# Loading the last 64 rows of three weight matrices: one transfer over 128 partitions, or two over 64

## The chip, the cores and the metric

The kernel runs on one core of a Trainium2 chip. The metric is device time in microseconds (us) of one execution; lower is better. A core has a matrix engine (PE in the profile), a vector engine (DVE), a scalar engine (ACT), GpSimd (POOL) and SyncE (SP). SP computes nothing here: it issues every transfer between the main memory and the on-chip buffer (SBUF, 128 partitions). Sixteen DMA engines carry the transfers.

## The reference

Two attention layers and two dense layers in turn, for one new token in each of 8 sequences. Both attention layers use the same weights and the same caches, and so do both dense layers.

```python
# x: 8 x 1 x 448 (bf16); 16 query heads, 8 key/value heads of size 256; the last 1024 positions of a cache of 4096
def A(x, k_cache, v_cache, wq, wo):          # wq 448 x 4096, wo 4096 x 448
    q = (x @ wq) per head; scores = q @ k.T * 256 ** -0.5
    return (softmax(scores) @ v) @ wo
def B(x, w1, w2):                             # w1 448 x 1792, w2 1792 x 448
    return silu(x @ w1) @ w2
x = x + A(layernorm(x)); x = x + B(layernorm(x))
x = x + A(layernorm(x)); x = x + B(layernorm(x))
```

## The kernel before

The first attention layer, the first dense layer and the second attention layer are computed sequence by sequence (b = 0 to 7), so that each K and V block is loaded once and used by both attention layers. The second dense layer comes once at the end, for all sequences together. In the code `layer1(b)` is the first attention layer of a sequence, `layer2(b)` the first dense layer (`chain`) and the second attention layer.

**Weights.** The inner dimension of wq, w1 and of each quarter of w2 is 448 = 3 x 128 + 64. The first 384 rows fill three column blocks of all 128 partitions. The last 64 rows fill a narrower block: its left half (output columns of the first half) lies in partitions 0 to 63, its right half in partitions 64 to 127. Two transfers of 64 partitions each bring that block, in each of `load_wq` (L411), `load_w1` (L419) and `load_w2` (L434).

**Loads.** All loads go through SP's queue in the order of the program: x, wq (three large and two small), the eight K blocks of sequence 0, w2 (four and two), wo (one), the eight V blocks of sequence 0, w1 (one and two), then for each next sequence eight K (L468) and eight V blocks (L480 and L474). A block is 512 KB. There are `R` = 30 slots for them; a load beyond the thirtieth waits until the PE has read the block that was in its slot.

**Compute.** DVE transposes each K block in its slot (L899). PE multiplies the queries by it (L639, in `scores`), DVE takes the maximum (L645) and turns it (L651 to L655), ACT takes the exponential (L659), PE transposes the result (L664) and multiplies it by V (L696, in `pv_rows`). PE then multiplies by wo (L765). In `chain`, PE multiplies by w1 (L518) and w2 (L793), and then by wq for the second layer's queries (L806). The very first use of wq is the projection for all eight sequences at the start (L511). Each transfer has a semaphore of its own; a product with wq, w1 or w2 waits for all transfers of that matrix (`WQ_R`, `W1_R`, `W2_R`).

**Order.** A planner (`Plan.schedule`) sets the order of the tasks on PE, DVE, ACT and POOL before the program is built. It simulates the engines with durations written in tables, and takes the ready task with the highest rank plus an entry of `BIAS`. `HOLD` says how long it holds an engine for a more urgent task, `PE_SCALE` stretches the PE's durations. The `rate` of a transfer (bytes per us) is the planner's guess of its speed and goes nowhere else. On the chip, each engine runs its list in that order, and semaphores make it wait.

Of the kernel before, what the change touches and what calls it, by code (L numbers as in the profile page):

```python
# [20 lines left out]
       "act:exp": 0.38, "act:oev": 0.30, "act:pTev": 0.20, "act:qrow": 0.51, "act:rowb": 0.50, "act:tanh": 0.22,  # L21
       "pool:pow": 0.53, "pool:pow8": 1.63}
SP_ISSUE, DMA_FIRST, DMA_LAST = 0.47, 1.2, 2.2
HOLD, PE_SCALE = 0.709, 1.049
BIAS = {"dve.KT.a": -15.4, "dve.max.a": -69.3, "dve.mT.a": -77.8, "act.exp.a": 32.3, "pe.l.a": 54.2,
        "pe.xinit.a": 20.0, "act.rsum.a": 23.2, "act..a": 109.1, "pe.oT.a": 45.0, "pe.wo.a": -2.4, "pe.stat.b":
        141.6, "pe.qturn.b": 64.2, "pe.qsel.b": 103.4, "pe.S1.0.b": 42.7, "pe.S1.1.b": 21.5, "dve.mg.c": -66.5,
        "act.exp.c": 37.9, "pe.l.c": -84.2, "pe.PV1.0.1.c": -85.8, "pe.PV1.0.3.c": 4.6, "pe.oT.c": -76.3,
        "dve.oTev.c": -102.8, "pe.PV1.1.2.c": -78.3}


class Task:
# [13 lines left out]
class Plan:  # L46
# [10 lines left out]
    def add(self, eng, fns, reads=(), writes=(), dur=0.1, prio=0.0, name="", n_bytes=0, dma_key=None):  # L57
        if not isinstance(fns, (list, tuple)):
            fns = [fns]
        if eng == "pool":  # L60
            writes = list(writes) + ["pool_serial"]
        t = Task(eng, list(fns), dur, prio, name, n_bytes)
        t.idx = len(self.tasks)
        t.sem = dma_key
        deps = {}

        def dep(o, raw):
            if o is not t:
                deps[o.idx] = (o, raw or (deps[o.idx][1] if o.idx in deps else False))

        for k in reads:
            if k in self.last_w:
                dep(self.last_w[k], True)
            if k[0] == "bank":
                for r in self.readers.get(k, ()):
                    if r.eng != eng:
                        dep(r, False)
        for k in writes:
            if k in self.last_w:
                dep(self.last_w[k], True)  # L80
            for r in self.readers.get(k, ()):
                dep(r, False)
        for k in reads:
            if k not in writes:
                self.readers.setdefault(k, []).append(t)
        for k in writes:
            self.last_w[k] = t
            self.readers[k] = []
        t.deps = deps
        self.tasks.append(t)  # L90
        return t

    def schedule(self):
# [15 lines left out]
        for t in reversed(tasks):  # L109
            r = max([u.rank + lag(t, u, raw) for u, raw in succ[t.idx]], default=0.0)  # L110
            t.rank = occ[t.idx] + r
            if t.eng == "sp":
                t.rank += DMA_FIRST + DMA_LAST
                if t.idx in following:
                    t.rank = max(t.rank, occ[t.idx] + following[t.idx].rank)
        urgency = [t.rank + BIAS.get(t.kind, 0.0) for t in tasks]

# [132 lines left out]
def bass_interleave_layers__sliding_block_cached__dense_activation_silu__decode_kernel(  # L250
    nc, A_x, A_k_cache, A_v_cache, A_wq, A_wo, B_x, B_w1, B_w2, out
):
    NB, Sq, D = A_x.shape
    _, HKV, SK, DH = A_k_cache.shape
    HD = A_wq.shape[1]
    H = HD // DH
    F = B_w1.shape[1]
    W = min(4096, max(256, SK // 4))
    S0 = SK - W
    P = 128  # L260
    assert NB == 8 and Sq == 1 and DH == 256 and H == 16 and HKV == 8 and W == 1024 and D == 448 and F == 1792
    KC = 4
    HD2, F2 = HD // 2, F // 2
# [13 lines left out]
    wq_sb = sb("wq_sb", [P, 3 * HD + HD2], BF16)  # L277
    wo_sb = sb("wo_sb", [P, NCH * DP], BF16)
    w1_sb = sb("w1_sb", [P, 3 * F + F2], BF16)
# [64 lines left out]
    def bk(i):  # L344
        return [("bank", i)]
# [7 lines left out]
    def act(fn, reads, writes, dur, prio, name=""):  # L353
        add("act", fn, reads=reads, writes=writes, dur=dur - LAT["act"], prio=prio, name=name)

    def pe(fns, reads, writes, shape, prio, name=""):

        n = len(fns) if isinstance(fns, (list, tuple)) else 1
        add("pe", fns, reads=reads, writes=writes, dur=n * max(0.0265, shape[0] / shape[1] / 2230.0), prio=prio,
            name=name)  # L360
# [40 lines left out]
    def dma(fn, writes, n_bytes, key, reads=(), rate=411.2e3):  # L401
        add("sp", fn, reads=reads, writes=writes, n_bytes=n_bytes, dma_key=key, dur=n_bytes / rate, name=key)
# [3 lines left out]
    def load_wq():  # L406
        for c in range(3):
            dma(lambda e, c=c: e.dma_start(wq_sb[:, c * HD:(c + 1) * HD], A_wq[c * P:(c + 1) * P, :]),
                [("wq", c)], P * HD * 2, "wq%d" % c, rate=410e3)
        for h in range(2):  # L410
            dma(lambda e, h=h: e.dma_start(wq_sb[64 * h:64 * h + 64, 3 * HD:], A_wq[3 * P:D, h * HD2:(h + 1) * HD2]),  # L411
                [("wq", 3 + h)], 32 * HD * 2, "wq%d" % (3 + h), rate=250e3)

    def load_w1():
        dma(lambda e: e.dma_start(w1_sb[:, 0:3 * F].rearrange("p (c n) -> p c n", c=3),
                                  B_w1[0:3 * P, :].rearrange("(c p) n -> p c n", p=P)),
            [("w1", 0)], 3 * P * F * 2, "w1", rate=390e3)
        for h in range(2):
            dma(lambda e, h=h: e.dma_start(w1_sb[64 * h:64 * h + 64, 3 * F:], B_w1[3 * P:D, h * F2:(h + 1) * F2]),  # L419
                [("w1", 1 + h)], 32 * F * 2, "w1%d" % h, rate=250e3)  # L420

    def load_wo():
        dma(lambda e: e.dma_start(wo_sb[:].rearrange("p (c n) -> p c n", n=DP)[:, :, 0:D],
# [2 lines left out]
    def load_w2():  # L426
        rows = w2_sb[:].rearrange("p (c n) -> p c n", n=DP)[:, :, 0:D]
        parts = B_w2.rearrange("(j r) n -> j r n", j=4)
        for j in range(4):
            dma(lambda e, j=j: e.dma_start(rows[:, 3 * j:3 * j + 3, :],  # L430
                                           parts[j, 0:3 * P, :].rearrange("(c p) n -> p c n", p=P)),
                [("w2", j)], 3 * P * D * 2, "w2%d" % j, rate=400e3)
        for h in range(2):
            dma(lambda e, h=h: e.dma_start(rows[64 * h:64 * h + 64, 12:14, :],  # L434
                                           parts[h:4:2, 3 * P:D, :].rearrange("j p n -> p j n")),
                [("w2", 4 + h)], P * D * 2, "w2%d" % (4 + h), rate=250e3)

    WO_R = ["wo"] + [("wo_s", g) for g in range(8)]
    W2_R = [("w2", j) for j in range(6)] + [("w2_s", g) for g in range(4)]
# [1 line left out]
    def row_sums(w, key, groups, prio):  # L441

        needs = ([("w2", j) for j in range(6)] if key == "w2" else [key]) + H8
        for g, (i0, i1) in enumerate(groups):
# [10 lines left out]
            else:  # L455
                for i in range(i0, i1):
# [2 lines left out]
                        accum_out=row[:, i - i0:i - i0 + 1]), needs, ["rowb", ("sums", key, g)], 0.75, prio, "rsum")  # L459
                act(lambda e, view=view, n=n, row=row: e.activation(view[:, :, D], row[:, 0:n], ACTF.Copy),  # L460
                    [("sums", key, g)], [(key + "_s", g)], 0.22, prio)
    WQ_R = [("wq", c) for c in range(KC + 1)]
    W1_R = [("w1", c) for c in range(3)]

    slot_of = {}

# [38 lines left out]
    def proj(bank_i, col, outs, lhs, half, rhs, n):  # L505

        fns = []
        for o in outs:
            for i in range(KC):
                r = rhs(xcol(i, o // half))  # L510
                fns.append(lambda e, o=o, i=i, r=r: e.matmul(  # L511
                    bank[bank_i][:, col + (o - outs[0]) * n:col + (o - outs[0] + 1) * n], lhs(o, i), r,
                    start=(i == 0), stop=(i == KC - 1)))
        return fns

    def up(x, nb, bi, col, reads, prio, fresh):
# [3 lines left out]
            tile_position=(0, 32 * j), skip_group_check=True) for c in range(KC) for j in range(4)],  # L520
           reads + W1_R, bk(XB) + ["part"], (D, 4), prio, "w1")
        if nb == 1:
# [48 lines left out]
    def start_rows(prio):  # L571
# [18 lines left out]
        pe(proj(YB, 0, range(NCH), wq_l, 16, lambda i: xh[:, i, :], 2 * NB),  # L590
           H8 + WQ_R, bk(YB), (2 * NB, 1), prio, "q1")
        yv = bank[YB][:, 0:2 * NCH * NB].rearrange("p (c n) -> p c n", n=2 * NB)
# [190 lines left out]
    def chain(b, prio):  # L783
# [20 lines left out]
        for k2 in range(2):  # L804
# [4 lines left out]
                start=(c == 0), stop=(c == KC - 1), tile_position=(0, 32 * j), skip_group_check=True)  # L809
                for c in range(KC) for j in range(4)], ["xbt"] + WQ_R, bk(wb), (512, 4), prio, "wq")  # L810
            act(lambda e, wb=wb: e.activation(qrow[:], bank[wb][:], ACTF.Copy),  # L811
# [56 lines left out]


    load_wq()  # L870
    start_rows(-10)

# [4 lines left out]
    def pump():  # L877

        while n_load[0] < len(seq) and (n_load[0] < R or seq[n_load[0] - R] in freed):
            x = seq[n_load[0]]  # L880
            slot_of[x] = n_load[0] % R
            n_load[0] += 1
            (load_k if x[1] == "k" else load_v)(slot_of[x], x[0], x[2])
            if x == (0, "k", 7):
                load_w2()
                load_wo()
            if x == (0, "v", 7):
                load_w1()
# [81 lines left out]
```

## Time and profile before

| | |
|---|---|
| median of 3 runs | 269.94 us (268.32 to 271.89) |
| the profiled execution | 270.87 us |
| its span, first to last instruction | 268.7 us |
| busy: PE, DVE, ACT, POOL | 190.6, 151.1, 89.1, 12.8 us |
| moved by the DMA engines | 78.21 MB, mean 291 GB/s |
| mean granted PE clock | 0.942 of full speed |

The profiled execution is 2.17 us longer than its span. All times below with a start are counted from the start of the span. The 40 slices of the page's second part are 6.7 us each. A row of stretches gives the length of the stretch, the busy time of each engine with the number of its instructions in brackets, the PE's clock, the share of the 16 DMA engines' time in which packets were under way, and the GB/s moved. A transfer's "landing" is the time from its issue by SP to its completion.

### The profile page before, as it was taken

To read this page: it belongs to the slowest core of one execution; us is meant where nothing else is said; L and a number is where in the kernel's file an instruction comes from. 1 tells how busy PE (TensorE), PEld (TensorE's weight loads), DVE (VectorE), ACT (ScalarE), POOL (GpSimd) and SP (SyncE) were. 2 spreads that over 40 slices of the span, in tenths; PEclk is the share of its full clock that TensorE was granted. 3 is DMA by queue.
4 is the path that set the end of the run, shared out by engine and by line. 5 is a ranking of instruction groups with operands and counts; after the bars stand their busy time and mean duration, and the time that the engine had idled before them with its cause. 6 is when DMAs were issued, how large, how long until landed. Compare 5 with 4: busy or idle time off the path is not lost.

```text
span 268.7 us, 8339 instructions
## 1 busy us (share of the span) xinstructions
PE 190.6 (71%) x3697; PEld 99.1 (37%) x3697; DVE 151.1 (56%) x410; ACT 89.1 (33%) x241; POOL 12.8 (5%) x25
## 2 busy tenths in 40 slices
PE   0062212398599977986997699689969986987663
PEld 0051100133345344444544444344435444433320
DVE  6369548619824973794686488449645862112211
ACT  2001347543133414433342443215233423230221
POOL 1200000000000000000000000000000000000020
PEclk9999999999959999999999999999988997995795
DMA  6999999999999999998999999899989984000000
GB/s 250 337 404 371 298 342 348 369 347 402 351 365 409 362 295 387 395 348 261 410 377 303 395 400 350 235 378 388 329 246 406 371 258 144 2 2 2 0 2 1
DMA packets 50227, 78.21 MB, mean 291 GB/s; under 512 B 2304, under 2 KB 41104, under 8 KB 49808
## 3 DMA queue, kind: packets, MB, share of 16 engines
q1 hardware_dynamic: 50192, 77.68, 83.6%
q8 instruction: 29, 0.48, 0.7%
q14 instruction: 6, 0.05, 0.1%
HBM read 77.67 MB, written 0.01 MB: 289 GB/s over the span
## 4 chain that ended last, share of the span: by engine, by line
PE 54%; SPq 19%; DMA 9%; DVE 8%; ACT 6%; issue 2%; POOL 1%; DVEq 0%; ACTq 0%
PE bank L696 11%; PE bank L639 10%; DMA slot<-in_A_k_cache_dram 9%; SPq L480 6%; PE bank L806 5%; SPq L430 5%; PE bank L772 5%; PE bank L765 5%; SPq L468 3%; SPq L474 3%; PE bank L518 3%; DVE mseg L645 2%; ACT qbd L659 2%; PE bank L793 2%; ACT qrow L811 2%
## 5 line engine op out<-in xcount | busy, mean ns | idle before, releaser
L899 DVE STREAM_TRANSPOSE slot<-slot 128x512 uint32<-128x512 uint32 x128 | 81.9, 684 | 9.3 <-DMA slot<-in_A_k_cache_dram 9.2
L696 PE MATMUL bank<-slot,pT_sb 128*2 128x256 bf16 x960 | 43.0, 307 | 9.6 <-DMA slot<-in_A_v_cache_dram 8.6
L639 PE MATMUL bank<-slot,qbd 128*8 128x256 bf16 x1024 | 42.0, 296 | 10.6 <-DVE slot L899 6.4
L696 PEld LDWEIGHTS bank<-slot,pT_sb 128*2 128x2 bf16 x960 | 21.6, 89 | 23.7 <-DMA slot<-in_A_v_cache_dram 9.0
L639 PEld LDWEIGHTS bank<-slot,qbd 128*8 128x8 bf16 x1024 | 21.8, 88 | 21.6 <-DVE slot L899 7.9
L659 ACT ACTIVATE qbd<-bank,mseg 128x256 bf16<-128x256 f32 x32 | 13.2, 472 | 41.7 <-DVE mseg L655 27.5
L664 PE MATMUL bank<-ident,qbd 128*128 128x128 bf16 x64 | 7.2, 249 | 23.4 <-ACT qbd L659 23.4
L704 ACT ACTIVATE qbd<-bank 128x256 bf16<-128x256 f32 x32 | 12.3, 384 | 29.4 <-PE bank L696 24.0
L765 PE MATMUL bank<-wo_sb,oT 128*1 128x449 bf16 x256 | 20.0, 368 | 0.0
L772 PE MATMUL bank<-wq_sb,cols_b 128*128 128x512 bf16 x64 | 19.4, 384 | 0.0
L645 DVE TENSOR_REDUCE mseg<-bank 128x1 f32<-128x256 f32 x32 | 13.2, 415 | 10.9 <-PE bank L639 10.4
L750 POOL TENSOR_TENSOR rhalf<-var,nhalf 128x1 f32<-128x1 f32 x16 | 8.7, 543 | 222.4 <-ACT var L748 222.4
L710 DVE TENSOR_TENSOR oT<-bank,l_sb 128x16 bf16<-128x16 f32 (+1 forms) x32 | 5.8, 195 | 22.2 <-PE bank L706 22.2
L608 ACT ACTIVATE qbd<-bank,mask 128x128 bf16<-128x128 f32 x32 | 12.2, 381 | 17.2 <-PE bank L603 16.4
L806 PE MATMUL bank<-wq_sb,xbt 128*1 128x512 bf16 x256 | 17.4, 393 | 0.6 <-DVE xbt L739 0.6
L677 DVE TENSOR_REDUCE l_sb<-bank 128x16 f32<-128x64 f32 x16 | 3.3, 205 | 24.4 <-PE bank L672 24.4
L664 PEld LDWEIGHTS bank<-ident,qbd 128*128 128x128 bf16 x64 | 4.3, 109 | 27.4 <-ACT qbd L659 26.9
L811 ACT ACTIVATE qrow<-bank 128x512 bf16<-128x512 f32 x16 | 9.6, 597 | 9.6 <-PE bank L806 9.6
L449 DVE TENSOR_REDUCE qbd<-wo_sb 128x5 f32<-128x2240 bf16 x4 | 9.7, 2479 | 2.6 <-DMA wo_sb<-in_A_wo_dram 2.6
L622 DVE TENSOR_TENSOR qbd<-bank,maskr 128x256 bf16<-128x256 f32 x16 | 6.8, 422 | 7.6 <-PE bank L617 7.6
L778 ACT ACTIVATE qrow<-bank 128x449 bf16<-128x449 f32 x8 | 4.4, 550 | 18.5 <-PE bank L765 18.5
L778 ACT ACTIVATE qrow<-bank,rhalf 128x449 bf16<-128x449 f32 x8 | 5.1, 640 | 11.3 <-PE bank L793 11.3
(133 smaller groups left out, 204.6 us busy)
## 6 DMA issues: line engine op xcount, KB each, us to landing
slot<-in_A_k_cache_dram SPq DMA_DIRECT2D x64, 512.0 KB, 10.5
slot<-in_A_v_cache_dram SPq DMA_DIRECT2D x64, 512.0 KB, 8.7
wo_sb<-in_A_wo_dram SPq DMA_DIRECT2D x1, 3584.0 KB, 17.9
wq_sb<-in_A_wq_dram SPq DMA_DIRECT2D x3, 1024.0 KB, 6.9
w_sb<-in_B_w_dram SPq DMA_DIRECT2D x4, 336.0 KB, 16.0
w_sb<-in_B_w_dram SPq DMA_DIRECT2D x1, 1344.0 KB, 11.5
wq_sb<-in_A_wq_dram SPq DMA_DIRECT2D x2, 256.0 KB, 10.3
w_sb<-in_B_w_dram SPq DMA_DIRECT2D x4, 112.0 KB, 9.5
```

The source lines that it names most:

```text
L430: dma(lambda e, j=j: e.dma_start(rows[:, 3 * j:3 * j + 3, :], parts[j, 0:3 * P, :].rearrange("(c p) n -> p c n", p=P)), [("w2", j)], 3 * P ...
L480: dma(lambda e: e.dma_start(slots[s][:, :].rearrange("v (j n) -> v j n", j=4), src.rearrange("j (v uh) d -> v j (uh d)", uh=2)), [("slot", ...
L639: fns.append(lambda e, cb=cb, par=par, j=j, kvh=kvh, kv=kv: e.matmul(bank[sc][32 * j:32 * j + 8, k2 * 256:(k2 + 1) * 256], qbd[qi][:, kvh, ...
L645: dve(lambda e: e.tensor_reduce(mseg[layer][:, k2:k2 + 1], bank[sc][:, k2 * 256:(k2 + 1) * 256], AX.X, ALU.max, negate=True), bk(sc), [("m ...
L659: act(lambda e, k2=k2: e.activation(e_sb[ei][:, k2, :, :].rearrange("p uh (jj ul) -> p uh jj ul", ul=4), bank[sc][:, k2 * 256:(k2 + 1) * 2 ...
L696: fns.append(lambda e, q=q, uh=uh, j=j, vv=vv: e.matmul(bank[ob][32 * j:32 * j + 2, c0:c0 + DH], pT_sb[ei][:, k2 * 2 + uh, j * 8 + 2 * q:j ...
L704: act(lambda e: e.activation(o_t, bank[ob][:, c0:c0 + DH], ACTF.Copy), bk(ob), [("qbd", ei, k2)], 0.42, prio, "oev")
L765: fns.append(lambda e, i=i, c=c, kvh=kvh: e.matmul(bank[XB][32 * c:32 * c + 1, 0:D1], oT1[:, i % 2, i // 2:i // 2 + 1], wo_sb[:, i * DP:i ...
L772: pe([lambda e: e.matmul(bank[SC[1]][:], zero_b.broadcast_to([P, P]), wq_sb[:, 0:512], start=False, stop=True, skip_group_check=True) for ...
L806: pe([lambda e, j=j, c=c, k2=k2, wb=wb: e.matmul(bank[wb][32 * j:32 * j + 1, :], xbt[:, xcol(c, k2):xcol(c, k2) + 1], wq_sb[:, c * HD + (( ...
L811: act(lambda e, wb=wb: e.activation(qrow[:], bank[wb][:], ACTF.Copy), bk(wb), ["rowb"], 0.55, prio, "qrow")
L899: dve(lambda e, v=v: e.transpose(v, v), [("slot", s)], [("slot", s)], 0.67, prio, "KT")
```

## The change

Each pair of 64-partition transfers for wq and w1 becomes one transfer over all 128 partitions. In main memory the two halves of a row lie next to each other, so the source is addressed as (half, row, column): 2 x 64 x 2048 elements for wq, 2 x 64 x 896 for w1. For w2 there are still two transfers, but each now covers 128 partitions and one column block, with a source of 2 x 64 x 448, instead of 64 partitions and two column blocks. The lists of semaphores to wait for become shorter by one for wq and w1. The planner's `BIAS`, `HOLD`, `PE_SCALE` and rates change as well.

```diff
-HOLD, PE_SCALE = 0.709, 1.049
-BIAS = {"dve.KT.a": -15.4, "dve.max.a": -69.3, "dve.mT.a": -77.8, "act.exp.a": 32.3, "pe.l.a": 54.2,
...
+HOLD, PE_SCALE = 0.659, 1.047
+BIAS = {"dve.KT.a": -21.1, "pe.S0.0.a": -50.7, "dve.max.a": -100.8, "dve.mT.a": -157.3, "act.exp.a": 42.6,
...
-        for h in range(2):
-            dma(lambda e, h=h: e.dma_start(wq_sb[64 * h:64 * h + 64, 3 * HD:], A_wq[3 * P:D, h * HD2:(h + 1) * HD2]),
-                [("wq", 3 + h)], 32 * HD * 2, "wq%d" % (3 + h), rate=250e3)
+        dma(lambda e: e.dma_start(wq_sb[:, 3 * HD:], A_wq[3 * P:D, :].rearrange("r (h n) -> h r n", h=2)),
+            [("wq", 3)], 64 * HD * 2, "wq3")
...
-        for h in range(2):
-            dma(lambda e, h=h: e.dma_start(w1_sb[64 * h:64 * h + 64, 3 * F:], B_w1[3 * P:D, h * F2:(h + 1) * F2]),
-                [("w1", 1 + h)], 32 * F * 2, "w1%d" % h, rate=250e3)
+        dma(lambda e: e.dma_start(w1_sb[:, 3 * F:], B_w1[3 * P:D, :].rearrange("r (h n) -> h r n", h=2)),
+            [("w1", 1)], 64 * F * 2, "w11", rate=390e3)
...
-        for h in range(2):
-            dma(lambda e, h=h: e.dma_start(rows[64 * h:64 * h + 64, 12:14, :],
-                                           parts[h:4:2, 3 * P:D, :].rearrange("j p n -> p j n")),
-                [("w2", 4 + h)], P * D * 2, "w2%d" % (4 + h), rate=250e3)
+        for i in range(2):
+            dma(lambda e, i=i: e.dma_start(rows[:, 12 + i, :], parts[2 * i:2 * i + 2, 3 * P:D, :]),
+                [("w2", 4 + i)], P * D * 2, "w2%d" % (4 + i), rate=350e3)
...
-    WQ_R = [("wq", c) for c in range(KC + 1)]
-    W1_R = [("w1", c) for c in range(3)]
+    WQ_R = [("wq", c) for c in range(KC)]
+    W1_R = [("w1", c) for c in range(2)]
```

Lines behind the change have numbers smaller by 4 in the changed kernel (L895 is what was L899). SP's queue before, from the first wq transfer to the second group of K blocks; the shape is that of the destination, partitions first:

```order
L408 DMA wq_sb<-in_A_wq_dram 128x4096 x3
L411 DMA wq_sb<-in_A_wq_dram 64x2048 x2
L468 DMA slot<-in_A_k_cache_dram 128x2048 x8
L430 DMA w_sb<-in_B_w_dram 128x3x448 x4
L434 DMA w_sb<-in_B_w_dram 64x2x448 x2
L423 DMA wo_sb<-in_A_wo_dram 128x32x448
L480 DMA slot<-in_A_v_cache_dram 128x4x512 x4
L474 DMA slot<-in_A_v_cache_dram 128x4x512 x4
L415 DMA w_sb<-in_B_w_dram 128x3x1792
L419 DMA w_sb<-in_B_w_dram 64x896 x2
L468 DMA slot<-in_A_k_cache_dram 128x2048 x8
```

The same place in the changed kernel:

```order
L407 DMA wq_sb<-in_A_wq_dram 128x4096 x3
L409 DMA wq_sb<-in_A_wq_dram 128x1x2048
L464 DMA slot<-in_A_k_cache_dram 128x2048 x8
L427 DMA w_sb<-in_B_w_dram 128x3x448 x4
L431 DMA w_sb<-in_B_w_dram 128x1x448 x2
L420 DMA wo_sb<-in_A_wo_dram 128x32x448
L476 DMA slot<-in_A_v_cache_dram 128x4x512 x4
L470 DMA slot<-in_A_v_cache_dram 128x4x512 x4
L413 DMA w_sb<-in_B_w_dram 128x3x1792
L416 DMA w_sb<-in_B_w_dram 128x1x896
L464 DMA slot<-in_A_k_cache_dram 128x2048 x8
```

The order of the loads is the same. The three tails are now over 128 partitions, with a middle dimension of 1 where the source has its three levels.

PE's order is the same up to the scores of sequence 1. There, before the change (L639 scores, L664 transposes of the exponentials, L696 products with V, L672 row sums of the exponentials):

```order
L617 MATMUL bank<-qT,sel 128x8x2 x4
L639 MATMUL bank<-slot,qbd 8x256 x88
L664 MATMUL bank<-ident,qbd 128x128 x4
L696 MATMUL bank<-slot,pT_sb 2x256 x32
L672 MATMUL bank<-pT_sb,cols_b 128x64 x2
L664 MATMUL bank<-ident,qbd 128x128 x4
L696 MATMUL bank<-slot,pT_sb 2x256 x16
```

And after it:

```order
L613 MATMUL bank<-qT,sel 128x8x2 x4
L635 MATMUL bank<-slot,qbd 8x256 x56
L660 MATMUL bank<-ident,qbd 128x128 x4
L635 MATMUL bank<-slot,qbd 8x256 x32
L692 MATMUL bank<-slot,pT_sb 2x256 x16
L668 MATMUL bank<-pT_sb,cols_b 128x64 x2
L692 MATMUL bank<-slot,pT_sb 2x256 x32
```

The last 32 score products of sequence 1's first layer have moved behind the first group of transposes, that of sequence 0's second layer. From there on the two orders differ in this manner in every sequence: the same instructions, with groups interleaved a little differently.

DVE at the same place, before (L645 maximum, L651, L652 and L655 the turning of it, L899 the transpose of a K block):

```order
L645 TENSOR_REDUCE mseg<-bank 128x1
L651 STREAM_TRANSPOSE mT<-mseg 128x32
L899 STREAM_TRANSPOSE slot<-slot 128x512 x2
L652 TENSOR_REDUCE mg<-mT 128x2
L655 STREAM_TRANSPOSE mseg<-mg 128x32
```

And after:

```order
L641 TENSOR_REDUCE mseg<-bank 128x1
L647 STREAM_TRANSPOSE mT<-mseg 128x32
L648 TENSOR_REDUCE mg<-mT 128x2
L651 STREAM_TRANSPOSE mseg<-mg 128x32
L895 STREAM_TRANSPOSE slot<-slot 128x512 x2
```

Two transposes of K blocks have moved behind the end of the turning.

More of the change, by code (lines that the diff above doesn't have):

```diff
@@ L23 @@
 SP_ISSUE, DMA_FIRST, DMA_LAST = 0.47, 1.2, 2.2
-HOLD, PE_SCALE = 0.709, 1.049
-BIAS = {"dve.KT.a": -15.4, "dve.max.a": -69.3, "dve.mT.a": -77.8, "act.exp.a": 32.3, "pe.l.a": 54.2,
[L26 to L29, printed above, removed]
+HOLD, PE_SCALE = 0.659, 1.047
+BIAS = {"dve.KT.a": -21.1, "pe.S0.0.a": -50.7, "dve.max.a": -100.8, "dve.mT.a": -157.3, "act.exp.a": 42.6,
+        "pe.l.a": 92.7, "act.rsum.a": 10.1, "act..a": 91.5, "pe.oT.a": 59.7, "pe.stat.b": 238.1, "pe.qturn.b":
+        161.5, "pe.qsel.b": 164.5, "pe.S1.1.b": 132.0, "act.exp.c": 71.3, "pe.PV1.0.2.c": -22.5, "act.oev.c":
+        90.3, "pe.oT.c": -39.1, "pe.PV1.1.2.c": -85.6}
 class Task:
```

## The prediction

> **What bounds the kernel now.** I read the page's slices first, to see which engine is full where. Slices are 6.7 us.
>
> ```profile
> span 268.7 us, 8339 instructions
> ...
> PE   0062212398599977986997699689969986987663
> ...
> DMA  6999999999999999998999999899989984000000
> GB/s 250 337 404 371 298 342 348 369 347 402 351 365 409 362 295 387 395 348 261 410 377 303 395 400 350 235 378 388 329 246 406 371 258 144 2 2 2 0 2 1
> ```
>
> In the first eight slices PE is mostly idle and the DMA engines are full: the start waits for loads. From the ninth PE is busy 6 to 9 tenths, and DMA is still full. The tail (from slice 35) has no loads. All transfers that change lie in the first 60 us. So I asked for the waits up to 60 us, for the chain that ended last around the second sequence's K blocks, and for SP's own waits after 100 us.
>
> ```profile
> ACT qrow L457 <- DMA w_sb<-in_B_w_dram: 9.5, 1, 9.5
> ...
> PE bank L696 <- DMA slot<-in_A_v_cache_dram: 8.6, 5, 4.7
> ...
> PE bank L511 <- DMA wq_sb<-in_A_wq_dram: 6.7, 1, 6.7
> ```
>
> ```profile
> 53.02 15.96 DMA slot<-in_A_k_cache_dram
> ...
> 69.00 0.71 DVE slot L899
> ```
>
> ```profile
> SPq L480 <- PE bank L529: 33.6, 5, 7.3
> SPq L474 <- PE bank L639: 25.8, 5, 5.9
> ```
>
> Up to 69 us compute waits for DMA: ACT's row sums for w2, PE for wq and for V, DVE for sequence 1's K. After 100 us SP waits for PE to free a slot: loads follow compute. So a delay of the first loads delays compute, and compute then hands out slots late by as much: nothing behind it makes up for it. Likewise a gain at the start is kept.
>
> Does w1 matter, which comes last of the weights? PE's rows in order of time, at its first use:
>
> ```profile
> 58.86 0.25 PE L745 MATMUL bank<-xbt 128*128 128x1 bf16 x4 [0.32 <-DVE xbt L739]
> 59.12 0.93 PE L518 MATMUL bank<-w_sb,xbt 128*1 128x448 bf16 x16
> ```
>
> ```profile
> L415 SPq DMA_DIRECT2D w_sb<-in_B_w_dram x1: 1418/1418/1418, 46.3 to 46.3; - x1
> ...
> DMA to landing us min/median/max: 11.5/11.5/11.5
> ```
>
> ```profile
> L419 SPq DMA_DIRECT2D w_sb<-in_B_w_dram x2: 598/825/1052, 47.8 to 48.9; - x2
> ...
> DMA to landing us min/median/max: 10.1/10.4/10.8
> ```
>
> w1's main part lands at 46.3 + 11.5 = 57.8 us, its last half at 48.9 + 10.1 = 59.0, and PE starts on it at 59.12. It has 0.1 us to spare. Any delay here is late on PE.
>
> **What the tails cost now.** The same for wq and w2:
>
> ```profile
> L408 SPq DMA_DIRECT2D wq_sb<-in_A_wq_dram x3: 365/424/427, 1.2 to 2.1; - x3
> ...
> DMA to landing us min/median/max: 4.9/6.9/9.5
> ```
>
> ```profile
> L411 SPq DMA_DIRECT2D wq_sb<-in_A_wq_dram x2: 587/631/675, 2.5 to 3.3; - x2
> ...
> DMA to landing us min/median/max: 10.1/10.3/10.6
> ```
>
> ```profile
> L430 SPq DMA_DIRECT2D w_sb<-in_B_w_dram x4: 901/3600/4915, 8.5 to 19.2; - x4
> ...
> DMA to landing us min/median/max: 10.8/16.0/17.7
> ```
>
> ```profile
> L434 SPq DMA_DIRECT2D w_sb<-in_B_w_dram x2: 608/998/1388, 21.7 to 23.1; - x2
> ...
> DMA to landing us min/median/max: 7.9/8.4/9.0
> ```
>
> wq's main part lands at 2.1 + 9.5 = 11.6, its tail at 3.3 + 10.6 = 13.9: 2.3 us. w2: 19.2 + 10.8 = 30.0 to 23.1 + 7.9 = 31.0: 1.0 us. w1: 57.8 to 59.0: 1.2 us. Together **4.5 us**, all on the path.
>
> **What they cost after.** Speeds come from stretches in which one kind of transfer runs: wq's tail, K, wo (rows of 896 bytes, as in w2), the main part of w1, its tail.
>
> ```profile
> 11.60:13.80 2.20, 0.00 (x0) 0.00 (x0) 0.00 (x0) 0.00 (x0) 0.00 (x0) 1.00 1.02 264
> 14.00:24.00 10.00, 5.53 (x166) 4.69 (x166) 8.12 (x13) 1.51 (x4) 0.00 (x0) 1.00 1.03 402
> ...
> 29.50:39.50 10.00, 1.51 (x18) 0.59 (x10) 5.54 (x10) 5.44 (x17) 0.00 (x0) 1.00 1.10 336
> ...
> 52.50:55.50 3.00, 3.00 (x42) 1.26 (x36) 0.17 (x1) 0.38 (x1) 0.00 (x0) 1.00 1.05 390
> 55.50:57.00 1.50, 1.50 (x36) 0.78 (x32) 0.16 (x1) 0.00 (x0) 0.00 (x0) 1.00 1.01 265
> ```
>
> Transfers over 64 partitions run at 264 and 265 GB/s, over 128 at 402 (K), 336 (wo) and 390 (w1). What no row shows is how a transfer is spread over the 16 engines when its source opens with a dimension of 2 (2 x 64 rows) and its destination with 128. All large transfers here open with the same 128 or 64 on both sides. There are two ends.
>
> *All 16 engines.* wq 524,288 bytes at 402 GB/s are 1.3 us, w2 and w1 229,376 bytes each at 336 and 390 GB/s 0.7 and 0.6: 2.6 in place of 4.5, a gain of 1.9 us.
>
> *Two engines, one for each half.* One engine's speed is a sixteenth of the row's: 25.1 GB/s for wq, 21.0 for 896-byte rows. wq: 262,144 bytes each, 10.4 us. w2: 57,344 bytes each, 2.7 us, twice 5.5. w1: 114,688 bytes in rows of 1,792 bytes, between 24.4 and 21.0 GB/s, 4.7 to 5.5, so 5.1. Together 21.0, **16.5 us more** than now. The other fourteen engines can run ahead, but every following K, V and wo transfer also has its share on these two, behind the tail, and is complete only with that share.
>
> The nearest row is that of the two transfers that open with a number other than 128 or 64, x and the result, with 8 rows:
>
> ```profile
> qbd<-in_A_x_dram SPq DMA_DIRECT2D x1, 7.0 KB
> out_dram<-qbd SPq DMA_DIRECT2D x1, 7.0 KB
> ```
>
> They alone of all issues have no landing behind their size. That fits a transfer which does not complete on sixteen engines, so that the opening dimension sets the number; it does not prove it. With it I take two engines.
>
> [...]
>
> From the 16.5 I take 2 off. A landing is that of the slowest engine: the packets of w1's tail start between 55.5 and 57 (the 265 GB/s row), yet it lands at 59.0, so the average engine is 2 us ahead of the slowest. If the two loaded engines are average ones, the loss is 14.5; if they are the slowest, 16.5. Average is likelier, with two picked of sixteen.
>
> **The order.** What moves is seen at the second sequence:
>
> ```profile
> 72.15 1.26 DVE L899 STREAM_TRANSPOSE slot<-slot 128x512 uint32<-128x512 uint32 x2
> 73.34 0.12 DVE L652 TENSOR_REDUCE mg<-mT 128x2 f32<-128x8 f32 x1
> ```
>
> ```profile
> 74.07 1.88 PE L639 MATMUL bank<-slot,qbd 128*8 128x256 bf16 x32 [2.55 <-DVE mseg L645]
> 75.88 0.61 PE L664 MATMUL bank<-ident,qbd 128*128 128x128 bf16 x4
> ```
>
> PE idles 2.55 us before the 32 scores. In the new order the two K transposes (1.26 us) stand behind L652, so the exponentials start 1.2 us sooner, and the four transposes (0.61 us) fall into PE's idle time. The scores come later by the two small DVE instructions put ahead of the K transposes. The bounds are the 2.55 us, gained or lost once; I take a gain of 0.5, since PE's lists hold the same work. SP has two issues fewer of 0.6 us each (the L411 and L419 rows). It queues about 10 us ahead of the landings there, so I cost them at nothing; without that cover they would be 1.2 us.
>
> **The sum.** 270.87 (the profiled execution: span 268.7, 2.17 around it) + 16.5 - 2 - 0.5 = 284.9, so **285 us**. The median of the three runs, 269.94, lies 0.9 below this execution, inside their spread.
>
> **The rivals.** *A, sixteen engines (not slower):* if the transfer is spread by its 128 destination partitions, the two halves' 4.5 us become 2.6 and the 16.5 never arise. It decides at wq's tail: landed at about 12.9 us it is A, past 20 us it is not. Time 270.87 - 1.9 - 0.5 = 268.5. For it speaks that every 128-partition row above runs at 336 GB/s or more, against it the 8-row transfers. With the largest gain of the order, 2.55, in two or three of the later sequences as well, A would reach 262.
>
> *B, the delay is made up.* The loop's stretches differ:
>
> ```profile
> 148.50:171.00 22.50, 20.54 (x433) 10.73 (x433) 14.88 (x39) 8.80 (x24) 1.08 (x2) 1.00 1.00 356
> 171.00:197.00 26.00, 21.05 (x441) 10.79 (x433) 16.27 (x45) 8.97 (x24) 1.08 (x2) 1.00 0.99 335
> ```
>
> If a changed meeting of loads and slots let the longer ones run like the shorter, 3.5 us in a stretch, two of them would give 7 back: 278. Against it: SP's waits on PE show loads following compute, which has no shorter list.
>
> *C, the change does less than it says.* w2 still has two transfers, so only wq and w1 save an issue; in A this is already counted.
>
> **How the numbers follow.** The forecast has a chance of 0.82, B 0.04, A near 268 us 0.10, A with the order's full gain 0.04. Two per cent (5.4 us) is about what a measurement of this kernel tells from no change. So slower 0.86, within 2% 0.10, faster 0.04. The range of the forecast goes from 285 up by the 2 us of the slowest engine and the order's 3 (0.5 taken back, 2.55 lost) to 290, with 1 for the spread between runs 291; down by 2 of the order, 7 of B and 1 of spread to 275. It leaves out A.
>
> **What would show it.** wq's tail lands near 22 us in place of 13.9 and PE's first wq product (L511) starts there, not at 14; sequence 0's K blocks land from about 23 us on, still 1.3 apart; somewhere between 15 and 45 us the DMA digits fall well under 9, as fourteen engines run dry; w1's tail lands near 73 and L518's row starts there; SP's waits for PE stay as they are. A tail landing by 13 us would make the prediction wrong in its main step; a late w1 with an unchanged end would make the carrying-through wrong.

## The result, and the profile after

| | before | after |
|---|---|---|
| median of 4 runs | 270.91 us (268.32 to 273.42) | 292.79 us (289.30 to 295.43) |
| ratio, 95% interval | | 1.075 (1.056 to 1.094) |
| span of the profiled execution | 268.7 us | 287.2 us |

The change makes the kernel 7.5% slower, about 20 us. The ratio leaves disturbed runs out, so it is not the quotient of the medians. The forecast was 285 us, with a range up to 291: the sign and the place were right, the size was too small.

The slices of the page after the change (now 7.2 us each) show where:

```profile
span 287.2 us, 8334 instructions
...
PE   0001440134588689699869769978996996987673
...
DMA  6997439999997999899999999989999997000000
GB/s 253 373 268 192 142 94 326 332 350 339 325 350 256 347 412 354 257 390 382 291 322 409 349 306 408 365 266 368 392 332 344 408 351 230 3 2 2 0 2 1
```

In the fourth to sixth slice (21 to 43 us) DMA falls to 7, 4 and 3 tenths and 192, 142 and 94 GB/s, where it was full before. PE starts its long busy part two to three slices later. Behind that the rows look as before. The transfers, from the page's list of issues (KB each, then the time to landing where there is one):

```profile
wq_sb<-in_A_wq_dram SPq DMA_DIRECT2D x3, 1024.0 KB, 6.9
w_sb<-in_B_w_dram SPq DMA_DIRECT2D x1, 1344.0 KB, 11.6
wq_sb<-in_A_wq_dram SPq DMA_DIRECT2D x1, 512.0 KB
w_sb<-in_B_w_dram SPq DMA_DIRECT2D x2, 112.0 KB
```

The changed transfers have no landing any more, like the 8-row transfers of before. When they are complete is read from what waits for them: PE's first product with wq, DVE's first transpose of a K block, ACT's first row sum of w2, and PE's first product with w1, in the rows in order of time:

```profile
27.85 3.56 PE L507 MATMUL bank<-qbd,wq_sb 128*128 128x16 bf16 x128 [20.48 <-DMA wq_sb<-in_A_wq_dram]
```

```profile
28.76 2.05 DVE L895 STREAM_TRANSPOSE slot<-slot 128x512 uint32<-128x512 uint32 x3 [17.27 <-DMA slot<-in_A_k_cache_dram]
```

```profile
47.45 0.58 ACT L453 ACTIVATE qrow<-w_sb 128x448 bf16<-128x448 bf16 x1 [12.02 <-DMA w_sb<-in_B_w_dram]
```

```profile
75.79 0.25 PE L741 MATMUL bank<-xbt 128*128 128x1 bf16 x4 [0.33 <-DVE xbt L735]
79.95 0.54 PE L514 MATMUL bank<-w_sb,xbt 128*1 128x448 bf16 x4 [3.91 <-DMA w_sb<-in_B_w_dram]
```

wq's first product comes at 27.85 us, the first K transpose at 28.76, w1's first product at 79.95, after a wait of 3.91 for w1 itself. Before, they came at 13.99, 15.64 and 59.12:

```profile
13.99 3.56 PE L511 MATMUL bank<-qbd,wq_sb 128*128 128x16 bf16 x128 [6.74 <-DMA wq_sb<-in_A_wq_dram]
```

```profile
15.64 2.05 DVE L899 STREAM_TRANSPOSE slot<-slot 128x512 uint32<-128x512 uint32 x3 [4.33 <-DMA slot<-in_A_k_cache_dram]
```

The shift is 13.9, 13.1 and 20.8 us at these three, and about 20 at the end by the ratio. (The two profiled spans differ by 18.5 us; the granted PE clock was 0.942 in the one before and 0.955 in the one after.)

What goes with the fall of the DMA digits is seen in SP's rows in order of time: the eight K blocks and the main part of w2, before and then after (start, time from the first issue to the end of the last, line):

```profile
3.89 4.53 SPq L468 DMA_DIRECT2D slot<-in_A_k_cache_dram  x8
8.47 13.14 SPq L430 DMA_DIRECT2D w_sb<-in_B_w_dram  x4
```

```profile
3.23 17.64 SPq L464 DMA_DIRECT2D slot<-in_A_k_cache_dram  x8
20.92 13.85 SPq L427 DMA_DIRECT2D w_sb<-in_B_w_dram  x4
```

The eight K issues took 4.53 us and now take 17.64, so w2 is issued 12.5 us later. The delay thus reaches the issuing engine too. From 32 to 34 us the DMA share is 0.13, two sixteenths: the other engines have run out of work by then. The semaphore updates in the trace show the same: a load of a K block raises its semaphore sixteen times. Fourteen of these are there by 12.6 us for the first block and by 26.5 for the eighth, the last two come at 27.3 and 28.7, and at 36.2 and 37.6. What holds SP back while it issues is not shown.

SP's waits after 110 us still name the same instructions of PE, so loads still follow compute:

```profile
SPq L476 <- PE bank L525: 31.1, 5, 6.9
SPq L470 <- PE bank L635: 30.5, 6, 6.0
```

### The profile page after: what moved, and what is told of

It reads as the page before. It is cut to its first block, busy times and chain, and to the rows that moved or that the text cites. A ratio compares the mean times of both kernels' runs of the same rounds, so it can differ in the third digit from the quotient of the medians.

```text
span 287.2 us, 8334 instructions
## 1 busy us (share of the span) xinstructions
PE 187.9 (65%) x3697; PEld 98.2 (34%) x3697; DVE 151.2 (53%) x410; ACT 88.6 (31%) x241; POOL 12.8 (4%) x25
## 4 chain that ended last, share of the span: by engine, by line
PE 47%; SPq 22%; DMA 12%; DVE 8%; ACT 6%; issue 2%; POOL 1%; DVEq 0%; ACTq 0%
PE bank L635 10%; PE bank L692 8%; DMA slot<-in_A_k_cache_dram 7%; SPq L464 6%; DMA w_sb<-in_B_w_dram 6%; SPq L476 5%; PE bank L802 5%; SPq L427 5%; PE bank L768 4%; PE bank L761 4%; PE bank L514 3%; SPq L470 3%; ACT qbd L655 2%; DVE mseg L641 2%; PE bank L789 2%
## 5 line engine op out<-in xcount | busy, mean ns | idle before, releaser
L895 DVE STREAM_TRANSPOSE slot<-slot 128x512 uint32<-128x512 uint32 x128 | 81.7, 685 | 25.6 <-DMA slot<-in_A_k_cache_dram 25.5
L692 PE MATMUL bank<-slot,pT_sb 128*2 128x256 bf16 x960 | 40.0, 287 | 10.4 <-DMA slot<-in_A_v_cache_dram 9.1
L635 PE MATMUL bank<-slot,qbd 128*8 128x256 bf16 x1024 | 40.6, 291 | 8.1 <-DVE slot L895 6.1
L692 PEld LDWEIGHTS bank<-slot,pT_sb 128*2 128x2 bf16 x960 | 20.0, 84 | 22.8 <-DMA slot<-in_A_v_cache_dram 8.9
L655 ACT ACTIVATE qbd<-bank,mseg 128x256 bf16<-128x256 f32 x32 | 13.1, 471 | 40.5 <-DVE mseg L651 26.5
L660 PE MATMUL bank<-ident,qbd 128*128 128x128 bf16 x64 | 6.6, 227 | 28.3 <-ACT qbd L655 28.3
L768 PE MATMUL bank<-wq_sb,cols_b 128*128 128x512 bf16 x64 | 20.2, 399 | 0.0
L507 PE MATMUL bank<-qbd,wq_sb 128*128 128x16 bf16 x128 | 3.6, 174 | 20.5 <-DMA wq_sb<-in_A_wq_dram 20.5
L660 PEld LDWEIGHTS bank<-ident,qbd 128*128 128x128 bf16 x64 | 3.7, 100 | 32.3 <-ACT qbd L655 32.1
L514 PE MATMUL bank<-w_sb,xbt 128*1 128x448 bf16 x128 | 8.2, 379 | 3.9 <-DMA w_sb<-in_B_w_dram 3.9
## 6 DMA issues: line engine op xcount, KB each, us to landing
w_sb<-in_B_w_dram SPq DMA_DIRECT2D x1, 1344.0 KB, 11.6
```

The costliest lines, as they stand in the source:

```text
L514: pe([lambda e, c=c, j=j: e.matmul(bank[XB][32 * j:32 * j + nb, 0:D], x(xcol(c, j // 2)), w1_r(j, c), start=(c == 0), stop=(c == KC - 1), ...
L635: fns.append(lambda e, cb=cb, par=par, j=j, kvh=kvh, kv=kv: e.matmul(bank[sc][32 * j:32 * j + 8, k2 * 256:(k2 + 1) * 256], qbd[qi][:, kvh, ...
L655: act(lambda e, k2=k2: e.activation(e_sb[ei][:, k2, :, :].rearrange("p uh (jj ul) -> p uh jj ul", ul=4), bank[sc][:, k2 * 256:(k2 + 1) * 2 ...
L692: fns.append(lambda e, q=q, uh=uh, j=j, vv=vv: e.matmul(bank[ob][32 * j:32 * j + 2, c0:c0 + DH], pT_sb[ei][:, k2 * 2 + uh, j * 8 + 2 * q:j ...
L768: pe([lambda e: e.matmul(bank[SC[1]][:], zero_b.broadcast_to([P, P]), wq_sb[:, 0:512], start=False, stop=True, skip_group_check=True) for ...
L895: dve(lambda e, v=v: e.transpose(v, v), [("slot", s)], [("slot", s)], 0.67, prio, "KT")
```

## The experiments

The ratios below are each to the kernel before, run beside it on the same chip. In all runs but the first of them, the order on PE, DVE, ACT and POOL is that of before (in the three with an added wait for wq, a few rows of DVE and ACT differ).

### Which part: the order or the transfers

**Order only.** The new tables, the old pairs of transfers (with the new rates, so that the planner's lists are those of the changed kernel):

```diff
-        dma(lambda e: e.dma_start(wq_sb[:, 3 * HD:], A_wq[3 * P:D, :].rearrange("r (h n) -> h r n", h=2)), ...
+        for h in range(2):
+            dma(lambda e, h=h: e.dma_start(wq_sb[64 * h:64 * h + 64, 3 * HD:], A_wq[3 * P:D, h * HD2:(h + 1) * HD2]), ...
...
```

> The new order on PE, DVE and ACT with the old pairs of 64-partition transfers. Theory (the slowdown is the tails on two engines): the time stays within 1% of before, 268 to 271 us, and wq's first product starts at 14 us as before. Rival (the new order costs the 6 us by which the forecast fell short): 275 to 277 us.

Measured: median 270.04 us, ratio 0.999 (0.993 to 1.006). The order costs nothing that can be told from zero.

**Tails only.** The old tables and order, all three tails as in the change. (In this kernel and in the next two the planner is given 250e3 for each tail, so that its order is that of before.)

> The old order, with all three tails as in the change. Theory: all of the slowdown and the small gain of the order missing, so 20 to 23 us above before, about 292, with sequence 1's first K transpose near 81 us. Rival (the order costs part): 12 to 15 us above before, about 284.

Measured: 288.63 us, ratio 1.071 (1.062 to 1.080), or 19 us. The first K transpose of sequence 1, from DVE's rows in order of time:

```profile
80.67 1.46 DVE L896 STREAM_TRANSPOSE slot<-slot 128x512 uint32<-128x512 uint32 x2 [5.30 <-DMA slot<-in_A_k_cache_dram]
```

It comes at 80.67 us, and in the changed kernel at 80.90. Within the intervals, the transfers are the whole slowdown.

**wq's tail only.** The old order, and of the three only wq's tail as in the change.

> The old order, with wq's tail alone changed. Theory: wq's first product waits till about 28 us, as in the changed kernel, and the 13 to 14 us are carried through to the end: about 284. Rival (a later wait absorbs an early delay, only the last late load counts): 270 to 275.

Measured: 280.03 us, ratio 1.038 (1.027 to 1.049), 10 us. PE's rows:

```profile
27.56 3.56 PE L510 MATMUL bank<-qbd,wq_sb 128*128 128x16 bf16 x128 [20.30 <-DMA wq_sb<-in_A_wq_dram]
```

```profile
71.05 0.93 PE L517 MATMUL bank<-w_sb,xbt 128*1 128x448 bf16 x16
```

wq's product is 13.6 us late, w1's 11.9, the end 7 to 13 (the interval). The theory's 284 lies just above that interval (277 to 283); some 2 us are given back on the way, and where was not followed up. The rival, that an early delay is absorbed, is out.

**w2's and w1's tails only.** The reverse of the last one.

> The old order, with the tails of w2 and w1 changed and wq's as before. Theory: w2's tail 5 us longer and w1's 4.5 longer, together 9 to 10 us above before, about 280; with the wq-only kernel it adds up to the tails-only kernel. Rival (w1's delay is hidden behind V and wo): 5 us above before.

Measured: 278.79 us, ratio 1.027 (1.016 to 1.039), 7.4 us. That lies between theory and rival, and the interval, 4 to 10 us, holds both. PE's row of w1:

```profile
66.01 1.66 PE L516 MATMUL bank<-w_sb,xbt 128*1 128x448 bf16 x16 [3.74 <-DMA w_sb<-in_B_w_dram]
```

w1's product is 6.9 us late, which agrees with the end. The two parts, 10.1 and 7.4 us, add up to 17.5, against 19.1 for both; with intervals of 3 us to each side they agree.

### How many engines carry a tail

wq's tail is varied, with the same destination, the same bytes and the same row length of 4 KB. Only the source's opening dimension (its outermost one) changes. To have 4, 8 or 16 there, other rows of wq are read in place of the last 64.

```diff
-            A_wq[3 * P:D, :].rearrange("r (h n) -> h r n", h=2)
+            A_wq[0:132, :].rearrange("(h r) n -> h r n", h=4)[:, 0:32, 0:HD2]        # 4 x 32 rows
+            A_wq[0:144, :].rearrange("(h r) n -> h r n", h=16)[:, 0:8, 0:HD2]        # 16 x 8 rows
```

> wq's tail with a source of 4 x 32 rows, 8 KB apart, the same destination and bytes (other rows of wq). Theory (the opening dimension sets the number of engines): four engines carry it, half as long as with two: 5 to 8.5 us after 11.1, so the first product starts at 16.5 to 19.5 us, and still no landing is shown. Rival (the count is 2 or 16 whatever the opening, or the slowness is in the three-level pattern): 28 or 12.5 us.

> wq's tail with a source of 16 x 8 rows, 8 KB apart, the same destination and bytes (other rows of wq). Theory (the opening dimension sets the number of engines): sixteen engines, 1.3 to 2.1 us after 11.1, the first product at 12.5 to 13.3 us, the transfer has a landing again, and the time is 0 to 1 us under before, about 269. Rival (a three-level source is slow in itself): over 16 us, and 4 us or more above before.

Measured, from PE's rows of the 4 x 32 kernel and then of the 16 x 8 kernel, and from the page of the latter:

```profile
23.13 3.56 PE L510 MATMUL bank<-qbd,wq_sb 128*128 128x16 bf16 x128 [15.88 <-DMA wq_sb<-in_A_wq_dram]
```

```profile
13.55 3.56 PE L510 MATMUL bank<-qbd,wq_sb 128*128 128x16 bf16 x128 [6.29 <-DMA wq_sb<-in_A_wq_dram]
```

```profile
wq_sb<-in_A_wq_dram SPq DMA_DIRECT2D x1, 512.0 KB, 10.9
```

With 16 there is a landing again, and the product comes at 13.55, not at 28: three levels in the source are not what costs 14 us. It is still later than the expected 12.5 to 13.3. The time of that kernel is 270.22 us, ratio 0.997 (0.990 to 1.004). With 4 the product comes at 23.13, later than the expected 16.5 to 19.5. Four engines are faster than two, but far from twice as fast.

The cleanest count is in runs in which the tail has the DMA engines to itself (openings of 2, 4 and 8, each run once for its trace, like the 4 x 32 kernel above and the one with close rows below; their times are not compared). There, the first K load waits for wq's tail:

```diff
-            [("slot", s)], W * DH * 2, "slot%d" % s)
+            [("slot", s)], W * DH * 2, "slot%d" % s, reads=[("wq", 3)] if (b, kvh) == (0, 0) else ())
```

> wq's tail alone changed, and the first K load waits until it has landed, so that the tail runs without other transfers. Theory C (contention: in the changed kernel the other fourteen engines write K at the same time and slow the two): the tail takes 10 to 10.5 us after wq's main part, so wq's first product starts at 21.5 to 22 us. Theory P (its source rows of 4 KB lie 8 KB apart): about 28 us, as with wq's tail alone changed. The end is not read here, since the wait delays K as well.

> wq's tail with a source of 4 x 32 rows, and the first K load waits until it has landed (other rows of wq). [...] Theory E (an engine alone always has its 25 GB/s): 5.1 us, first product at 16.3 to 17 us.

> The same with 8 x 16 rows. [...] Theory E: 2.6 us, first product at about 14 us.

Stretches within the tail, for openings of 2, 4 and 8. The last two columns are the share of the 16 engines' time and GB/s:

```profile
13.00:16.00 3.00, 0.00 (x0) 0.00 (x0) 0.00 (x0) 0.00 (x0) 0.00 (x0) 1.00 0.13 55
```

```profile
13.00:16.00 3.00, 0.00 (x0) 0.00 (x0) 0.00 (x0) 0.00 (x0) 0.00 (x0) 1.00 0.25 89
```

```profile
11.50:13.00 1.50, 0.00 (x0) 0.00 (x0) 0.00 (x0) 0.00 (x0) 0.00 (x0) 1.00 0.50 139
```

The shares are 0.13, 0.25 and 0.50: two, four and eight sixteenths. **In these three kernels the number of engines is the opening dimension of the source**, though the destination opens with 128 in all of them. The semaphore updates in the changed kernel's trace count the same: the semaphore of wq's tail, with an opening of 2, is raised once at 3.6 us, just after the issue, and then twice, at 26.3 and 27.7, and that of x, with its 8 rows, once and then 8 times.

### Why wq's tail took 16.7 us and not 10.4

wq's main part lands at 2.1 + 9.0 = 11.1 us in the changed kernel (its last issue and landing):

```profile
L407 SPq DMA_DIRECT2D wq_sb<-in_A_wq_dram x3: 376/427/428, 1.2 to 2.1; - x3
...
DMA to landing us min/median/max: 4.9/6.9/9.0
```

So the tail took 27.85 - 11.1 = 16.7 us. Two theories: other traffic (C), or source rows 8 KB apart (P). The kernel with the tail alone tells for C. Against P stands this one, which reads 2 x 64 rows that lie 4 KB apart, beside K as in the change:

```diff
-            A_wq[3 * P:D, :].rearrange("r (h n) -> h r n", h=2)
+            A_wq.rearrange("r (h n) -> (r h) n", h=2)[0:130, :].rearrange("(a r) n -> a r n", a=2)[:, 0:64, :]
```

> wq's tail with a source of 2 x 64 rows that lie close together (4 KB apart) instead of 8 KB apart; it brings other rows of wq, so the result is another. Theory P: first product at 21.5 to 22 us. Theory C: 27 to 28 us, no change.

PE's rows, of the tail alone and of the close rows:

```profile
21.48 3.56 PE L510 MATMUL bank<-qbd,wq_sb 128*128 128x16 bf16 x128 [14.22 <-DMA wq_sb<-in_A_wq_dram]
```

```profile
27.91 3.56 PE L510 MATMUL bank<-qbd,wq_sb 128*128 128x16 bf16 x128 [20.65 <-DMA wq_sb<-in_A_wq_dram]
```

Alone, the tail takes 10.4 us, counted from the changed kernel's 11.1, as the prediction said. Close rows change nothing: 27.91 us, against 27.56 with wq's tail alone changed. So the other transfers slow the two engines, from about 25 GB/s each (262,144 bytes in 10.4 us) to 16 (in 16.7 us). In the tail's time the K loads run on the other fourteen (the fourteen early updates of each block), and they are slowed too. The stretches of the wq-only kernel:

```profile
13.00:16.00 3.00, 0.00 (x0) 0.00 (x0) 0.00 (x0) 0.00 (x0) 0.00 (x0) 1.00 1.01 258
16.00:21.00 5.00, 0.00 (x0) 0.00 (x0) 0.00 (x0) 0.00 (x0) 0.00 (x0) 1.00 1.04 280
```

All engines are shown busy, but they move 258 and 280 GB/s, 16 to 18 for each, where K alone moves 402, 25 for each. Nor do the loads gain by K running beside the tail: DVE's first row sums of wo, which wait for its load, come at 53.32 us with wq's tail changed and at 52.85 in the kernel that also holds K back.

What slows them is not shown. Theory E (25 GB/s for an engine alone, whatever their number) asked for 16.3 to 17 us with 4 engines and no other transfers, and for about 14 with 8. The products came later, at 18.08 and 15.56 us:

```profile
18.08 3.56 PE L510 MATMUL bank<-qbd,wq_sb 128*128 128x16 bf16 x128 [10.83 <-DMA wq_sb<-in_A_wq_dram]
```

```profile
15.56 3.56 PE L510 MATMUL bank<-qbd,wq_sb 128*128 128x16 bf16 x128 [8.30 <-DMA wq_sb<-in_A_wq_dram]
```

By the stretches one engine moves 27 GB/s in a group of two (55 / 2), 22 in one of four and 17 in one of eight. The rate of the four changes: in the same trace they move 74 GB/s from 11.5 to 13 us and 89 from 13 to 16, that is 18 and 22 each. The runs do not show why an engine moves less in a larger group.

### What one transfer is worth when all engines carry it

All four changed transfers with a source of 16 x 8 rows, and then with a source of 128 rows in one level, as a K load has it:

```diff
-            A_wq[3 * P:D, :].rearrange("r (h n) -> h r n", h=2)
+            A_wq[3 * P:D, :].rearrange("r (h n) -> (r h) n", h=2)      # w1 likewise
-            parts[2 * i:2 * i + 2, 3 * P:D, :]
+            B_w2[P * i:P * i + P, :]                                    # other rows of w2
```

> The old order, each of the four changed transfers over 128 partitions with a source of 16 x 8 rows (other rows of the same matrices): what the change would bring if all sixteen engines carried it. The prediction's rival A: 1.9 us under before, 0.993 of its time. [...]

> The old order, with the four changed transfers over 128 partitions whose source is 128 rows in one level, as in a K load. wq's and w1's tails bring the right bytes with the halves of a row in neighbouring partitions, w2's bring other rows, so the result is another. The prediction's rival A in its pure form: wq's tail 1.3 us after wq's main part (first product at 12.6 to 13.0 us), w2 and w1 0.3 and 0.6 us sooner, 1.9 us under before, 0.993. Rival (as with 16 x 8 rows, nothing is gained): first product at 13.5 us or later, 0.998 to 1.002.

Measured: 16 x 8 rows give 0.999 (0.994 to 1.005). 128 rows in one level give 0.994 (0.988 to 0.9995), the only kernel here that is faster than before, by 1.7 us: the interval just leaves out 1, and the gain is less than the 2% that the prediction counts as a change. PE's rows of the latter:

```profile
12.38 3.56 PE L508 MATMUL bank<-qbd,wq_sb 128*128 128x16 bf16 x128 [5.13 <-DMA wq_sb<-in_A_wq_dram]
```

```profile
57.10 0.93 PE L515 MATMUL bank<-w_sb,xbt 128*1 128x448 bf16 x16
```

wq's product is 1.6 us sooner than before, w1's 2.0. So one transfer over 128 partitions can be worth what rival A gave it, if its source is 128 rows in one level.

An opening of 16 is not enough for that, as the stretches in which wq's tail is under way show, first with 16 x 8 rows (wq's tail alone changed), then with 128 rows in one level (where the first K block follows within the stretch):

```profile
11.50:13.00 1.50, 0.00 (x0) 0.00 (x0) 0.00 (x0) 0.00 (x0) 0.00 (x0) 1.00 0.95 243
```

```profile
11.50:13.00 1.50, 0.62 (x24) 0.65 (x25) 0.00 (x0) 0.00 (x0) 0.00 (x0) 1.00 1.04 418
```

Nearly all of the engines' time is taken in both, but 16 x 8 rows move 243 GB/s, no more than the old pairs (264), and one level 418. Whether the third level or the share of the partitions that each engine gets makes this difference was not tested. What spoils the change is thus first the source's opening dimension, which leaves two engines; but with sixteen engines the form of 16 x 8 rows gained nothing either.

A kernel with this layout and the right result needs the last 64 values of x in neighbouring pairs of partitions, everywhere that x is turned into columns. That was not tried.

## Why the prediction was right or wrong, point by point

- **The bound, and what is carried through: right.** w1's product is 20.8 us late in the changed kernel, and the end about 20; 6.9 and 7.4 with w2 and w1 alone; 11.9 and 10.1 with wq alone.
- **Two engines: right.** The number was the author's estimate, from the missing landings of the 8-row transfers, which were the right hint; no run of the kernel before shows a count of 2. The shares 0.13, 0.25 and 0.50 show it.
- **wq's term, 10.4 us: too small, and nearly the whole miss.** It measured 16.7. The step that failed is "one engine's speed is a sixteenth of the row's". That row (402 GB/s) is one in which all sixteen engines carry K. Alone, two engines keep its 25 GB/s each, but here the other fourteen carry K beside them, and each of the two moves only 16. The prediction said that these "can run ahead", and gave no price to what that does to the two. With 6.3 more, 285 becomes 291.3; before's 270.87 times 1.075 is 291.2. That these agree to a tenth is luck: the interval of the ratio is 286 to 296 us.
- **w2's and w1's terms: about right.** w2's main part lands at 41.6 us by the semaphore updates in the trace and ACT starts on w2 at 47.45, 5.9 us against 5.5. w1's tail took 79.95 - 74.1 (the main part lands at 62.5 + 11.6) = 5.8 us against 5.1. With w2 and w1 changed alone, their price at w1's product was 6.9 us, against (5.5 + 5.1) - 2.2 = 8.4, or 6.4 with the whole of the 2 for the slowest engine taken off.
- **The 2 us off for the slowest engine: right in size, its reason not shown.** With the tails as measured, 16.7 for wq, 5.9 for w2 and 5.8 for w1, the extra over 4.5 is 24, and 20.8 arrived. No run tells where the 3 us went, or whether the two engines are average ones.
- **The order, 0.5 us gained: not told from zero** (0.999, 0.993 to 1.006). The prediction priced SP's two fewer issues at nothing, and did not foresee that the eight K issues grow from 4.5 to 17.6 us; no run here separates what that alone costs.
- **Rival A:** the mechanism does not hold for this change. Its price of 1.9 us was met by a source of 128 rows in one level (0.994 measured, 0.993 expected), and not by 16 x 8 rows, which all engines carry as well (0.999). **Rival B**, the delay made up, did not happen. **C** is contained in A, as the prediction says.
- **The signs named:** the fall of the DMA digits came between 21 and 43 us, as said, and SP's waits for PE stayed. wq's product came at 27.85, not 22, and the first K transpose at 28.76, where K was to land from about 23 us: both are the miss in wq's tail, 6 us. The K blocks then landed 1.2 to 1.3 us apart by the semaphore updates, as said. w1's product came at 79.95, not 73, which is 7 us.

## What to carry to other kernels

Look at the outermost dimension of a transfer's source before counting partitions: here a source that opened with 2 left fourteen of sixteen DMA engines out (a share of 0.13), and the K blocks and w2 behind it in the queue waited for those two. With an opening of 16 nearly all of the engines' time was taken (0.95), but they moved 243 GB/s; 128 rows in one level moved 418. It showed here as a transfer without a landing in the profile, a DMA share of 0.13, two sixteenths, and a fall from 402 to 258 GB/s with all engines shown busy. Where a few engines are loaded beside others, take their speed from a stretch with the same mix: here 16 GB/s each, where 25 was assumed.

## What the runs showed of the hardware that was not expected

With a three-level source, engines that carry a lone transfer did not keep their speed as their number grew: 27 GB/s each for two, 22 for four, 17 for eight, and 15 for sixteen (243 / 16, with K behind the tail in the queue), in the stretches above. With a source in one level sixteen moved 26 each (418 / 16). And two engines with 512 KB take about 10 us alone but 16.7 beside K loads on the others, while four engines, with half as much each, take about 7 alone (18.08 - 11.1) and 12 beside K (23.13 - 11.1).
